# Loading q and k through casting transfers, and issuing row writes and transposes earlier, in a fused attention and MLP kernel

## Chip, cores, metric

One core of a Trainium2 chip. The metric is the device time of one execution in microseconds (us), the median of several runs. The five engines are named TensorE (PE in the profile, PEld for its weight loads), VectorE (DVE), ScalarE (ACT), GpSimd (POOL) and the sync engine (SP). SP computes nothing here; it issues transfers.

## The reference

Eight batches of eight heads, 576 tokens, head size 64, all float32. Causal attention with a decay bias comes first, then an MLP with exact GELU over all 4608 tokens.

```python
scores = scale * q @ k.T                      # per batch and head
bias   = -(cum[i] - cum[j]),  cum = cumsum(max(s, 0))
scores = where(causal, -1e9, scores + min(bias, 0))
attn   = softmax(scores);  o = attn @ v
x = o.transpose(0, 2, 1, 3).reshape(4608, 512)
y = gelu(x @ w_in) @ w_out                    # 512 -> 2048 -> 512
```

## The kernel before

The kernel works in chunks of 512 tokens. Chunk c runs the MLP of its tokens (layer 1, then layer 2) and, between the pieces of layer 2, the attention of batch c+1 (`nb`). Meanwhile the q and k of batch c+2 are prepared: loaded in float32, cast to bf16 (16 bit floats) on POOL with the two heads of a pair interleaved, written to memory as rows, and read back by transposing transfers into `qkT`. There are two `qkT` buffers, so batch c+2 takes the buffer that batch c had. Batches 0 and 1 take another way (casting loads and transposes on TensorE).

A "mask" below is VectorE's multiplication of the exponentials `P` of a block of scores by the triangle `tri_bf`; a transfer "lands" when the profile shows it complete.

The fast formula is valid only if q, k and v are small enough. A certificate checks this: `absmax` reduces each batch's `qkT`, and if the test at the end fails, a slow general branch computes everything again.

Each engine is given its instructions in the order in which the program writes them (no scheduler reorders them). What an instruction waits for is derived from the program order too.

```python
def load_qk(b, n, p0, p1, eng):                   # float32, 1536 byte runs, one slot each for q and k
    raws[b, n] = work.tile([PR, H, NR, D], fp32, tag=f"raw{n}", bufs=1, ...)
    eng.dma_start(out=raws[b, n]..., in_=...)
def cast(b, n, p, eng):                           # POOL: cast and interleave one head pair
    ... work.tile([PR, NP, NR, 2, D], bf16, tag="qkbf", bufs=2, ...)
    eng.tensor_copy(qk_of[b, i][:, p]..., raws[b, n][:, 2 * p : 2 * p + 2])
def write_rows(b, i, eng): ...                    # qk_bf -> rows in memory
def transpose_rows(b, p):                         # rows -> qkT, two transfers
    for i in range(2):
        nc.sync.dma_start_transpose(out=qkT[b % 2][:, i, p, :S], in_=rows_of[b, i][p])
def absmax(b, p):                                 # VectorE, for the certificate
    nc.vector.tensor_reduce(amx[:, b * NP + p], qkT[b % 2][:, :, p, :S], ...)

for c in range(NCH):
    nb = c + 1
    # ... first pieces of layer 1 ...
    if 0 < c and nb < B:
        if nb + 1 < B:
            load_v(nb + 1, [nc.sync])
            for i, n in enumerate("qk"):
                cast_next(nb + 1, n)              # casts, then loads q or k of batch nb+2 on POOL
                write_rows(nb + 1, i, nc.sync)
        scale_v(nb, STS, nc.vector)
        absmax_v(nb)
    # ...
    if c < B:
        for p in range(NP):
            absmax(c, p)
    for f2 in range(3, FT // 2):
        l1_item(c, f2)
    # ... c == 0 has its own order: tr_pair(1, p), load_qk(2), casts, rows and transposes of batch 2 ...
    elif nb < B:
        l2_item(c, 0, 0, 4); sc_item(nb, 0); l2_item(c, 0, 4)
        for p in range(1, NP):
            if nb + 1 < B:
                transpose_rows(nb + 1, p - 1)
            sc_item(nb, p); av_item(nb, p - 1)
            l2_item(c, p, 0, 12)                  # each finished l2 piece: copy to o_sb (3 buffers), store on SP
            # ... last p: transpose_rows(nb + 1, p), av_item(nb, p), norm_rest(nb) ...
            l2_item(c, p, 12)
```

## Time and profile before

| | before |
|---|---|
| median (lowest to highest of 3) | 351.07 us (350.35 to 351.12) |
| span of the profiled run, mean granted clock | 352.2 us, 0.985 |
| TensorE busy | 322.4 us |
| TensorE idle that is not start or tail | near 62, 88 to 95 and 182 us |
| length of chunks 1 to 6 | 41.7, 34.7, 37.8, 35.6, 34.6, 34.6 us |

A chunk's length is taken here from the start of its layer 1 in TensorE's timeline to the start of the next; 34.6 us is a chunk without a wait.

The page of the profile, the span and the engines' busy time:

```profile
span 352.2 us, 6309 instructions
...
PE 322.4 (92%) x2538; PEld 164.9 (47%) x2538; DVE 202.9 (58%) x363; ACT 202.2 (57%) x286; POOL 69.7 (20%) x98
```

The kernel is bound by TensorE, so only time in which TensorE stands still can be won. The view of waits for TensorE says what it stood still for (us in total, times, longest); the three largest lines that are not part of the start:

```profile
PE sc_ps L366 <- DMA qkT<-rows: 5.6, 2, 4.4
...
PE avr L394 <- DVE o_sb L498: 3.1, 1, 3.1
PE avd L394 <- DVE xT L427: 2.3, 1, 2.3
```

The table of stretches shows the first two with what follows: busy us of each engine (and instructions) in each stretch, then the granted clock, the DMA share and GB/s.

```profile
core 0: us, PE busy (x) PEld busy (x) DVE busy (x) ACT busy (x) POOL busy (x), PEclk, DMA share, GB/s
60.00:64.00 4.00, 0.94 (x24) 0.83 (x20) 4.00 (x6) 1.29 (x3) 3.70 (x5) 1.00 1.08 278
64.00:68.00 4.00, 4.00 (x39) 2.39 (x37) 3.96 (x6) 1.06 (x3) 3.37 (x5) 0.62 1.26 233
...
92.00:96.00 4.00, 0.58 (x8) 0.49 (x10) 0.00 (x0) 0.12 (x1) 0.00 (x0) 0.96 1.16 231
```

After a gap of some 3 us the clock was granted at 0.62 for the next 4 us, so a gap costs more than its length. In the first stretch VectorE and POOL are both busy nearly all the time: POOL casts. VectorE's timeline near the third gap shows what that does to a small mask (start, length, operation):

```profile
177.92 1.34 DVE L381 TENSOR_TENSOR P<-P,tri_bf 128x512 bf16<-128x512 bf16 x2 [0.69 <-ACT P L372]
179.18 3.70 DVE L386 TENSOR_TENSOR P<-P,tri_bf 128x128 bf16<-128x128 bf16 x1
182.81 0.41 DVE L427 SCALAR_TENSOR_TENSOR xT<-avn,ln 128x256 bf16<-128x256 f32 x1
```

This mask takes 0.22 us elsewhere. Here it took 3.70 us, to the end of four POOL casts in a row.

The groups of instructions of the reductions and of one half of the casts (busy us and mean ns, then idle time of the engine just before them and what ended it):

```profile
L203 DVE TENSOR_REDUCE amx<-qkT 128x2 f32<-128x1152 bf16 x32 | 40.9, 1335 | 0.0
...
L166 POOL CAST qk_bf<-raw_q 96x768 bf16<-96x768 f32 x24 | 20.1, 882 | 109.3 <-DMA rows<-qk_bf 102.5
```

The 0.0 on the first line is the one to remember: in the kernel before, VectorE never stood idle in front of a reduction.

Last, the transfers. The view of DMA queues from 40 to 43 us, while POOL's queue (q0: casting loads) and SP's queue (q1: v of batch 1 in 256 byte runs) are both full, gives packets, MB and share of the 16 engines:

```profile
q0 software_dynamic: 446, 0.48, 92.4%
q1 hardware_dynamic: 447, 0.11, 28.0%
```

The two queues moved packets in equal number, 446 against 447, as they would if they took turns packet by packet. A queue of small packets therefore gets little: 0.11 MB in 3 us. When POOL's queue had run empty (46 to 48 us), SP's moved 0.46 MB in 2 us.

### The profile page before, as it was taken

Reading aid. Unit: us, or ns where it says so; the run is one execution under the profiler, and the core shown is the slowest. Engines: PE = TensorE matmul, PEld = TensorE weight load, DVE = VectorE, ACT = ScalarE, POOL = GpSimd, SP = SyncE. Lnnn points to the kernel's source line nnn. Section 1 sums busy time; section 2 is a strip of 40 time slices with the busy share of each in tenths; the row PEclk is TensorE's granted clock in tenths of the full one; section 3 lists DMA queues with packets and bytes.
Section 4 is the critical chain, followed back from the end, with each engine's and each line's share of the span. In section 5 each row is a group of like instructions: output and inputs, shape, how many; then the busy total and the mean of one; then the engine's idle time right before and its main releaser. Section 6 shows DMA issues by size and latency. Waiting matters only on the chain.

```text
span 352.2 us, 6309 instructions
## 1 busy us (share of the span) xinstructions
PE 322.4 (92%) x2538; PEld 164.9 (47%) x2538; DVE 202.9 (58%) x363; ACT 202.2 (57%) x286; POOL 69.7 (20%) x98
## 2 busy tenths in 40 slices
PE   1778998798599999999979999999999999999993
PEld 1653454453255445544544455445544554444441
DVE  4596476889434985594579556865485548050011
ACT  2676628286365776667646676767576757403500
POOL 6581012705302600810080052000000000000000
PEclk9999999899989999999998999999999999999999
DMA  8999989995999999899989994862520100011011
GB/s 154 161 207 190 197 167 236 243 266 185 237 214 226 202 236 247 197 192 223 269 193 171 227 243 127 159 175 74 132 51 0 61 32 31 0 70 53 1 61 66
DMA packets 86516, 54.38 MB, mean 154 GB/s; under 512 B 67984, under 2 KB 78736, under 8 KB 86480
## 3 DMA queue, kind: packets, MB, share of 16 engines
q1 hardware_dynamic: 76752, 33.19, 42.9%
q0 software_dynamic: 9728, 20.71, 29.4%
q8 instruction: 22, 0.36, 0.4%
q14 instruction: 14, 0.11, 0.1%
HBM read 36.85 MB, written 16.52 MB: 152 GB/s over the span
## 4 chain that ended last, share of the span: by engine, by line
PE 79%; DMA 7%; DVE 6%; ACT 4%; issue 2%; SPq 1%; POOL 0%; DVEq 0%; ACTq 0%; POOLq 0%
PE o_ps L491 34%; PE h_ps L472 31%; PE sc_ps L366 5%; PE avn L394 3%; DMA rows<-qk_bf 3%; PE avd L394 3%; DMA qkT<-rows 2%; ACT P L372 2%; DVE vv L220 2%; DVE qkT L354 2%; DMA early_k<-in_k_dram 2%; PE avr L394 1%; PE tr_ps L349 1%; DVE P L381 1%; DVE P L386 1%
## 5 line engine op out<-in xcount | busy, mean ns | idle before, releaser
L491 PE MATMUL o_ps<-w_out_r,gT 128*128 128x512 bf16 x576 | 134.9, 384 | 0.0
L472 PE MATMUL h_ps<-xT,w_in_r 128*128 128x512 bf16 x576 | 127.3, 381 | 1.9 <-DVE xT L427 1.3
L472 PEld LDWEIGHTS <-w_in_r 128*128 128x128 bf16 x576 | 56.4, 98 | 70.8 <-issue 4.5
L372 ACT ACTIVATE P<-sc_ps 128x1024 bf16<-128x1024 f32 x64 | 62.0, 1021 | 47.9 <-PE sc_ps L366 47.7
L478 ACT ACTIVATE gT<-h_ps 128x1024 bf16<-128x1024 f32 x54 | 54.3, 1023 | 48.8 <-PE h_ps L472 48.7
L491 PEld LDWEIGHTS <-gT 128*128 128x128 bf16 x576 | 53.3, 98 | 61.5 <-issue 1.7
L498 DVE COPY o_sb<-o_ps 128x512 f32<-128x512 f32 x36 | 24.8, 688 | 57.9 <-PE o_ps L491 57.9
L381 DVE TENSOR_TENSOR P<-P,tri_bf 128x512 bf16<-128x512 bf16 x61 | 28.8, 475 | 49.0 <-ACT P L372 48.1
L166 POOL CAST qk_bf<-raw_q 96x768 bf16<-96x768 f32 x24 | 20.1, 882 | 109.3 <-DMA rows<-qk_bf 102.5
L203 DVE TENSOR_REDUCE amx<-qkT 128x2 f32<-128x1152 bf16 x32 | 40.9, 1335 | 0.0
L427 DVE SCALAR_TENSOR_TENSOR xT<-avn,ln 128x256 bf16<-128x256 f32 (+3 forms) x64 | 21.6, 384 | 23.3 <-ACT ln L412 23.3
L220 DVE TENSOR_TENSOR vv<-raw_v,wb 128x512 bf16<-128x512 f32 (+2 forms) x46 | 33.0, 775 | 0.0
L366 PE MATMUL sc_ps<-qkT 64*128 64x256 bf16 (+2 forms) x320 | 22.6, 267 | 9.3 <-DMA qkT<-rows 5.6
L411 ACT ACTIVATE ln<-avd 128x256 f32<-128x256 f32 x56 | 18.6, 390 | 15.2 <-PE avd L394 15.1
L366 PEld LDWEIGHTS <-qkT 64*128 64x128 bf16 x320 | 14.0, 99 | 24.2 <-issue 11.3
L412 ACT ACTIVATE ln<-ln 128x512 f32<-128x512 f32 (+1 forms) x40 | 23.5, 588 | 1.3
L394 PEld LDWEIGHTS <-vv 128*64 128x64 bf16 x384 | 18.2, 116 | 11.5 <-issue 7.7
L481 ACT ACTIVATE gT<-h_ps 128x512 bf16<-128x512 f32 x36 | 19.6, 602 | 6.3 <-PE h_ps L472 6.3
L210 DVE TENSOR_REDUCE amv<-raw_v 128x1 f32<-128x2048 f32 (+1 forms) x16 | 22.9, 1470 | 0.0
L166 POOL CAST qk_bf<-raw_k 96x768 bf16<-96x768 f32 x24 | 20.0, 880 | 0.6 <-DMA raw_k<-in_k_dram 0.6
L394 PEld LDWEIGHTS <-wb 128*64 128x64 bf16 x384 | 18.5, 117 | 2.9 <-issue 2.5
L394 PE MATMUL avd<-P,wb 128*64 128x256 bf16 x224 | 16.3, 269 | 2.3 <-DVE xT L427 2.3
(82 smaller groups left out, 154.6 us busy)
## 6 DMA issues: line engine op xcount, KB each, us to landing
out_dram<-o_sb SPq DMA_DIRECT2D x36, 256.0 KB, 2.7
raw_v<-in_v_dram SPq DMA_DIRECT2D x32, 256.0 KB, 6.7
raw_q<-in_q_dram POOLq DMA_DIRECT2D x6, 1152.0 KB, 8.6
raw_k<-in_k_dram POOLq DMA_DIRECT2D x6, 1152.0 KB, 12.3
rows<-qk_bf SPq DMA_DIRECT2D x12, 576.0 KB, 6.1
w_in_r<-in_moe_w_in_dram POOLq DMA_DIRECT2D x4, 512.0 KB, 8.0
w_out_r<-in_moe_w_out_dram POOLq DMA_DIRECT2D x4, 512.0 KB, 13.2
raw_v<-in_v_dram SPq DMA_DIRECT2D x8, 128.0 KB, 5.1
```

Of the source, the lines that this page charges most:

```text
L166: eng.tensor_copy(qk_of[b, i][:, p].rearrange("p r e d -> p e r d"), raws[b, n][:, 2 * p : 2 * p + 2])
L203: nc.vector.tensor_reduce(amx[:, b * NP + p], qkT[b % 2][:, :, p, :S], axis=AX, op=ALU.max, apply_absolute_value=True)
L220: eng.tensor_tensor(vb[:n_st, st0:st1, h0:h1, :], t[:n_st, st0:st1, h0:h1, :], wb[:n_st, st0:st1, b * H + h0 : b * H + h1] .unsqueeze(3).t ...
L366: nc.tensor.matmul(s_ps[:, e, off : off + n], lhsT=qkT[b % 2][e * 64 : e * 64 + 64, 1, p, jt * 128 : jt * 128 + 128], rhs=qkT[b % 2][e * 6 ...
L372: nc.scalar.activation(P[:, :, UO[u] : UO[u] + UW[u]], s_ps[:, :, : UW[u]], func=AF.Exp, scale=scale)
L381: eng.tensor_tensor(d, d, tri_bf.unsqueeze(1).unsqueeze(1).to_broadcast([128, 2, 2, 128]), op=MULT)
L394: nc.tensor.matmul(out[e * 64 : e * 64 + 64, lo : lo + n], lhsT=(wb[:, jt, b * H + h : b * H + h + 1].to_broadcast([128, 64]) if den else ...
L412: nc.scalar.activation(ln[:, :w], ln[:, :w], func=AF.Exp, scale=-1.0)
L472: nc.tensor.matmul(h_of[c, f2][i], lhsT=w_in_r[:, ko, ft * 128 : (ft + 1) * 128], rhs=xT[:, ko, c * NB % XW : c * NB % XW + NB], start=(ko ...
L478: nc.scalar.activation(gT_of[c][:, f2 * 2 : f2 * 2 + 2, :], hh_of[c, f2], func=AF.Gelu)
L491: nc.tensor.matmul(o_ps, lhsT=gT[:, ft, sub * 128 : (sub + 1) * 128], rhs=w_out_r[:, ft, :], start=(ft == 0), stop=(ft == FT - 1),)
L498: nc.vector.tensor_copy(o_sb, o_ps)
```

## The change

The intent: take the casts and the wide float32 loads away from POOL and the queues, and have batch c+2 ready earlier. All q and k come by the casting loads (2304 byte runs in memory, 1152 bytes in bf16), into three slots; POOL only interleaves head pairs, in bf16; batches 2 and 3 are loaded in the prologue; row writes and transposes are issued earlier. The core of the diff:

```diff
-    def load_qk(b, n, p0, p1, eng):            # float32 load, one slot
-    def cast(b, n, p, eng):                    # POOL cast, 4 per tensor
+    def load_qk(b):                            # casting loads, bufs=3
+        for p in (0, 2):
+            for n in "qk":
+                load_early(b, n, p, both=True)
+    def interleave(b, n):                      # POOL copy in bf16, 2 per tensor
 ...
+    for b in (2, 3):
+        load_qk(b)
+    for n in "qk":
+        interleave(2, n)
     for c in range(NCH):
 ...
             if nb + 1 < B:
                 load_v(nb + 1, [nc.sync])
                 for i, n in enumerate("qk"):
-                    cast_next(nb + 1, n)
+                    interleave(nb + 1, n)
                     write_rows(nb + 1, i, nc.sync)
+                if nb + 2 < B:
+                    load_qk(nb + 2)
+                for p in range(NP):
+                    transpose_rows(nb + 1, p)
             scale_v(nb, STS, nc.vector)
             absmax_v(nb)
 ...  (absmax(c, p) follows here, unchanged)
             for p in range(1, NP):
-                if nb + 1 < B:
-                    transpose_rows(nb + 1, p - 1)
                 sc_item(nb, p)
 ...  (chunk 0: both row writes of batch 2 right after load_v(2), its transposes in two places)
```

More of the change, by code (lines that the diff above doesn't have):

```diff
@@ L42 @@
     ST = 5
-    NR = 6
-    PR = S // NR
     SL = S - 512
@@ L99, in load_early @@
         src = q if n == "q" else k
-        if b == 0 and p == 0:
-            early[n] = work.tile([128, 2, 2, 2, G * D], bf16, tag=f"raw{n}", bufs=1, name=f"early_{n}")
+        if p == 0:
+            early[b, n] = work.tile([128, 2, 2, G * D], bf16, tag=f"raw{n}", bufs=3, name=f"early_{n}")
         e0 = (p // 2) * 64
-        out = early[n][e0 : e0 + 64, b, p % 2]
+        out = early[b, n][e0 : e0 + 64, p % 2]
         if both:
-            out = early[n][e0 : e0 + 64, b].rearrange("g j e f -> g (j e) f")
+            out = early[b, n][e0 : e0 + 64].rearrange("g j e f -> g (j e) f")
         ap = [[G * D, 64], [S * D, 4 if both else 2], [1, G * D]]
@@ L143 @@
     raws = {}
-    def load_qk(b, n, p0, p1, eng):
-        src = q if n == "q" else k
-        if p0 == 0:
-            raws[b, n] = work.tile([PR, H, NR, D], fp32, tag=f"raw{n}", bufs=1, name=f"raw_{n}")
-        eng.dma_start(
-            out=raws[b, n][:, 2 * p0 : 2 * p1].rearrange("p h r d -> p h (r d)"),
-            in_=bass.AP(
-                tensor=src.tensor,
-                offset=src.offset + b * H * S * D + 2 * p0 * S * D,
-                ap=[[NR * D, PR], [S * D, 2 * (p1 - p0)], [1, NR * D]],
-            ),
-        )
+    def load_qk(b):
+        for p in (0, 2):
+            for n in "qk":
+                load_early(b, n, p, both=True)
     qk_of = {}
-    def cast(b, n, p, eng):
+    def interleave(b, n):
         i = 0 if n == "q" else 1
-        if (b, i) not in qk_of:
-            qk_of[b, i] = work.tile([PR, NP, NR, 2, D], bf16, tag="qkbf", bufs=2, name="qk_bf")
-        eng.tensor_copy(
-            qk_of[b, i][:, p].rearrange("p r e d -> p e r d"), raws[b, n][:, 2 * p : 2 * p + 2]
-        )
+        t = qk_of[b, i] = work.tile([128, 2, G, 2, D], bf16, tag="qkbf", bufs=2, name="qk_bf")
+        for j in range(2):
+            nc.gpsimd.tensor_copy(
+                t[:, j].rearrange("g r e d -> g e r d"),
+                early[b, n][:, j].rearrange("g e (r d) -> g e r d", r=G),
+            )
     rows_of = {}
     def write_rows(b, i, eng):
-        rows_of[b, i] = t = dram.tile([NP, S, 128], bf16, name=f"rows{b}_{i}")
+        rows_of[b, i] = t = dram.tile([2, 2, S, 128], bf16, name=f"rows{b}_{i}")
         eng.dma_start(
-            out=t.rearrange("j (p r) c -> p j (r c)", r=NR),
+            out=t.rearrange("j a (g r) c -> (a g) j (r c)", r=G),
             in_=qk_of.pop((b, i)).rearrange("p j r e d -> p j (r e d)"),
@@ L180, in transpose_rows @@
         for i in range(2):
-            nc.sync.dma_start_transpose(out=qkT[b % 2][:, i, p, :S], in_=rows_of[b, i][p])
+            nc.sync.dma_start_transpose(out=qkT[b % 2][:, i, p, :S], in_=rows_of[b, i][p % 2, p // 2])
     def v_tile(b):
@@ L345, in tr_item @@
         e0 = (p // 2) * 64
-        src = early["qk"[i]]
+        src = early[b, "qk"[i]]
         for r in range(G):
@@ L350, in tr_item @@
                     t_ps[e * 64 : e * 64 + 64, r, :],
-                    src[e0 : e0 + 64, b, p % 2, e, r * D : (r + 1) * D],
+                    src[e0 : e0 + 64, p % 2, e, r * D : (r + 1) * D],
                     ident_bf[e0 : e0 + 64, e0 : e0 + 64],
@@ L503, in exp_set @@
         nc.scalar.preload_act_table_set("natural_log_exp_and_others")
-    def cast_next(b, n):
-        for p in range(NP):
-            cast(b, n, p, nc.gpsimd)
-        if b + 1 < B:
-            load_qk(b + 1, n, 0, NP, nc.gpsimd)
     load_v(0, [nc.sync])
@@ L551 @@
         load_w(1, i)
-    for p in (0, 2):
-        for n in "qk":
-            load_early(1, n, p, both=True)
+    load_qk(1)
     v_tile(1)
@@ L599 @@
             tr_pair(1, 3)
-            for n in "qk":
-                load_qk(2, n, 0, NP, nc.gpsimd)
             sc_item(1, 0)
@@ L604 @@
             load_v(2, [nc.sync])
-            for n in "qk":
-                cast_next(2, n)
+            for i in range(2):
+                write_rows(2, i, nc.sync)
             sc_item(1, 1)
@@ L615 @@
             l2_item(c, 3, 0, 4)
-            write_rows(2, 0, nc.sync)
+            for p in (0, 1):
+                transpose_rows(2, p)
             av_item(1, 0)
@@ L626 @@
             norm_rest(1)
-            write_rows(2, 1, nc.sync)
-            for p in range(NP):
+            for p in (2, 3):
                 transpose_rows(2, p)
@@ L643 @@
                 if p == NP - 1:
-                    if nb + 1 < B:
-                        transpose_rows(nb + 1, p)
                     av_item(nb, p)
```

## The prediction

> **What bounds it now.** TensorE: the page has it busy 322.4 us of a 352.2 us span (92%). From 113.5 us on, the chain of waits is almost wholly matmuls, 34.6 us per token chunk. What can be won:
> - (a) 60.9 to 63.9 us: TensorE waits 3.1 us for an output copy on VectorE, which POOL's casts slow (one 128x128 mask takes 0.84 us instead of 0.22). The granted clock is then 0.62 for 4 us (about 1.5 us).
> - (b) 88 to 95 us: 5.6 us for the transposes of batch 2. Their key rows, written at 74.2, landed 11.0 us later, behind the fp32 loads of batch 3. The clock falls to 0.62 again.
> - (c) 179 to 184 us: a mask waits 3.7 us, to the end of POOL's key casts; TensorE loses 3.2 us, the next chunk 1.0 us.
>
> The table by stretches has DMA near 1.0 from 24 to 221 us, so transfer order matters.
>
> **What changes.** TensorE, VectorE and ScalarE keep their order.
> - POOL: 48 casts of 0.88 us (768 elements) become 24 copies of 1152; by length 1.2 to 1.3 us each (estimate), 30 us instead of 40.
> - Loads: the same bytes are read, half written. Casting loads have 1152 byte packets (written), the fp32 loads 4.6 KB ones.
> - Loads of batches 2 and 3 follow batch 1's at once on POOL's queue, instead of waiting for 51 and 63 us.
> - SP issues rows of batch 2 right after v of batch 2, and in later chunks all eight transposes before the chunk's four output stores.
>
> **Critical path.**
> (b) goes: rows of batch 2 land near 73 us, transposes from 81, needed at 90. Gain 5.5 us.
> (c) probably goes: POOL's copies move to the start of the score phase, or before it. Gain 4 us; a contended mask may give back 1 to 2. The Trainium skill ("SBUF — State Buffer", Who interferes with whom: VectorE and GpSimd share a port pair under an exclusive lock) fits the stretched masks.
> (a) gets worse. The Trainium skill ("DMA: Bandwidth & Descriptors", Queues, rings and completion order) says that each engine round-robins between queues by packet. The trace agrees: from 34 to 46 us both queues moved about 460 packets in 3 us, so v of batch 1, in 256 byte packets, got 38 GB/s; alone (46 to 48 us) it got 0.46 MB in 2 us. Now POOL's queue stays full until about 62 us, and the last v tile lands near 61 to 62 instead of 50. VectorE, in order, waits for it at 58; TensorE resumes near 65 instead of 63.9, with the same clock dip. Loss 1 to 2 us.
> New: stores behind eight transposes. With three output buffers, in chunk 1 the fourth copy may wait for the first store's landing: 0 to 3 us.
>
> Sum: 351 − 5.5 − 4 + 1.5 + 1.5 ≈ 344.5 us. Range 338 to 351. Chances: faster 0.47, same 0.48, slower 0.05.
>
> **Right if:** no TensorE wait for transposes near 90 us; a wait of 4 us near 61 to 65 us, VectorE's v scaling waiting for its load; chunks of 34.6 us from 110 us on; no 3 us mask wait; POOL busy under 68 us.
>
> **Wrong if:** v of batch 1 lands as early as before (then nearer 341); stores hold VectorE and then TensorE for many us in chunks 1 to 4 (then 350); or POOL's copies are slower per element, or meet masks in every chunk.

## The result

| | before | after |
|---|---|---|
| median | 351.1 us (350.35 to 351.76, 4 runs) | 415.47 us (415.01 to 417.3, 4 runs) |
| ratio | | 1.1844 (95%: 1.1799 to 1.1888) |
| span, clock of the profiled run | 352.2 us, 0.985 | 413.2 us, 0.917 |
| start of chunk 1 | 71.6 us | 74.7 us |
| length of chunks 1 to 6 | 41.7, 34.7, 37.8, 35.6, 34.6, 34.6 us | 58.5, 48.0, 49.8, 42.3, 43.4, 34.6 us |

A ratio is the mean time of one kernel's fast runs over that of the other's of the same rounds, so not quite the ratio of the medians quoted. The change is 18% slower, far outside the predicted range.

The loss is in chunks 1 to 5: 16.8 + 13.3 + 12.0 + 6.8 + 8.8 = 57.7 of the 61.0 us by which the spans differ; another 3.1 us had been lost before chunk 1. These are the chunks in which the transposes of a later batch now stand ahead of the reductions (chunk 0 also transposes, but behind its reductions). Chunk 6, which prepares no batch, has its old length. TensorE's granted clock was lower there too, a mean of 0.83 to 0.92 over each of chunks 1 to 5 against 1.00 in chunk 6, so the loss contains some slower work besides waits.

The page after:

```profile
span 413.2 us, 6273 instructions
...
PE 326.3 (79%) x2496; PEld 169.7 (41%) x2538; DVE 191.2 (46%) x363; ACT 202.6 (49%) x286; POOL 61.7 (15%) x86
```

No engine was given more work than before (TensorE's busy time is 3.9 us longer, at the lower clock); all of them stand still more. The waits, all engines, the two lines that are new:

```profile
DVE amx L194 <- DMA qkT<-rows: 79.2, 17, 12.5
...
PE avn L385 <- DVE P L372: 58.9, 5, 22.3
```

TensorE waits 58.9 us in five waits for VectorE's masks, and VectorE waits 79.2 us in front of the reductions `amx`, for the transposes. The groups for the reductions and for one half of POOL's copies:

```profile
L194 DVE TENSOR_REDUCE amx<-qkT 128x2 f32<-128x1152 bf16 x32 | 42.1, 1346 | 79.2 <-DMA qkT<-rows 79.2
...
L156 POOL COPY qk_bf<-early_q 128x1152 bf16<-128x1152 bf16 x12 | 13.6, 1166 | 161.6 <-DMA rows<-qk_bf 156.9
```

The reductions are as many and as long as before (1346 against 1335 ns); the 0.0 of idle time has become 79.2. Chunk 2 shows how that reaches TensorE. VectorE's timeline there:

```profile
138.38 2.87 DVE L201 TENSOR_REDUCE amv<-raw_v 128x1 f32<-128x2048 f32 x2
149.40 1.35 DVE L194 TENSOR_REDUCE amx<-qkT 128x2 f32<-128x1152 bf16 x1 [8.14 <-DMA qkT<-rows]
154.84 1.35 DVE L194 TENSOR_REDUCE amx<-qkT 128x2 f32<-128x1152 bf16 x1 [4.09 <-DMA qkT<-rows]
160.93 2.61 DVE L194 TENSOR_REDUCE amx<-qkT 128x2 f32<-128x1152 bf16 x2 [4.74 <-DMA qkT<-rows]
163.46 0.75 DVE L372 TENSOR_TENSOR P<-P,tri_bf 128x512 bf16<-128x512 bf16 x2
```

The four reductions of chunk 2 run one by one as pairs of transposes land. Only then come the masks, which are next on VectorE and had nothing to do with the transposes. SP's timeline of the same chunk:

```profile
135.49 0.33 SPq L491 DMA_DIRECT2D out_dram<-o_sb  x1
135.87 4.64 SPq L183 DMA_DIRECT2D raw_v<-in_v_dram  x5
140.60 1.08 SPq L165 DMA_DIRECT2D rows<-qk_bf  x2
145.27 11.55 SPq L172 DMA_TRANSPOSE qkT<-rows  x8
164.97 18.81 SPq L491 DMA_DIRECT2D out_dram<-o_sb  x4
```

And the chain of waits:

```profile
148.79 2.71 PE o_ps L482 x12
...
151.81 9.03 DMA qkT<-rows
...
160.93 0.95 DVE amx L194
...
163.46 0.42 DVE P L372
...
163.93 0.95 PE avn L385 x8
```

So each chunk has become one chain: the last output store of the chunk before, v loads, rows written, rows landed, transposes, transposes landed, reductions, masks, and only then the rest of layer 2 (17.3 us, to 181.2), whose last store lets SP begin again. Transfers that were meant to be a chunk ahead are back on the critical path of the same chunk.

One part of the prediction can be read off directly: v of batch 1 starving behind POOL's queue, from 52 to 55 us.

```profile
q0 software_dynamic: 432, 0.47, 91.3%
q1 hardware_dynamic: 433, 0.11, 27.6%
```

VectorE's timeline has the v scaling waiting until 62.9 us (it was idle for the 3.52 us before, and "issue" stands there because the profile shows no releaser for it):

```profile
62.91 0.89 DVE L211 TENSOR_TENSOR vv<-raw_v,wb 128x512 bf16<-128x512 f32 x2 [3.52 <-issue]
```

### The profile page after: what moved, and what is told of

The parts are those of the page before. It is cut to its first block, busy times and chain, and to the rows that moved or that the text cites. A ratio compares the mean times of both kernels' runs of the same rounds, so it can differ in the third digit from the quotient of the medians.

```text
span 413.2 us, 6273 instructions
## 1 busy us (share of the span) xinstructions
PE 326.3 (79%) x2496; PEld 169.7 (41%) x2538; DVE 191.2 (46%) x363; ACT 202.6 (49%) x286; POOL 61.7 (15%) x86
## 4 chain that ended last, share of the span: by engine, by line
PE 62%; DMA 20%; SPq 9%; issue 3%; DVE 3%; POOL 1%; DVEq 0%
PE o_ps L482 27%; PE h_ps L463 25%; DMA qkT<-rows 8%; DMA raw_v<-in_v_dram 8%; SPq L172 5%; PE avn L385 4%; SPq L183 3%; DMA w_in_r<-in_moe_w_in_dram 3%; PE avd L385 3%; PE sc_ps L357 2%; DVE amx L194 2%; DMA rows<-qk_bf 1%; PE avr L385 1%; DVE P L372 1%; PE avw L385 1%
## 5 line engine op out<-in xcount | busy, mean ns | idle before, releaser
L482 PE MATMUL o_ps<-w_out_r,gT 128*128 128x512 bf16 x551 | 137.3, 393 | 2.7 <-issue 1.9
L463 PE MATMUL h_ps<-xT,w_in_r 128*128 128x512 bf16 x559 | 125.2, 379 | 3.1 <-DVE xT L418 1.7
L482 PEld LDWEIGHTS <-gT 128*128 128x128 bf16 x576 | 54.6, 101 | 65.7 <-issue 8.7
L194 DVE TENSOR_REDUCE amx<-qkT 128x2 f32<-128x1152 bf16 x32 | 42.1, 1346 | 79.2 <-DMA qkT<-rows 79.2
L385 PE MATMUL avn<-P,vv 128*64 128x256 bf16 x224 | 18.4, 291 | 63.4 <-DVE P L372 58.9
L385 PEld LDWEIGHTS <-vv 128*64 128x64 bf16 x384 | 20.3, 121 | 72.7 <-issue 65.2
L156 POOL COPY qk_bf<-early_q 128x1152 bf16<-128x1152 bf16 x12 | 13.6, 1166 | 161.6 <-DMA rows<-qk_bf 156.9
L372 DVE TENSOR_TENSOR P<-P,tri_bf 128x512 bf16<-128x512 bf16 x61 | 25.8, 441 | 21.7 <-ACT P L363 21.6
L211 DVE TENSOR_TENSOR vv<-raw_v,wb 128x512 bf16<-128x512 f32 (+2 forms) x46 | 26.8, 642 | 3.5 <-issue 3.5
L385 PEld LDWEIGHTS <-wb 128*64 128x64 bf16 x384 | 20.5, 125 | 0.3
L385 PE MATMUL avd<-P,wb 128*64 128x256 bf16 x224 | 18.1, 288 | 0.0
```

The source lines that it names most:

```text
L211: eng.tensor_tensor(vb[:n_st, st0:st1, h0:h1, :], t[:n_st, st0:st1, h0:h1, :], wb[:n_st, st0:st1, b * H + h0 : b * H + h1] .unsqueeze(3).t ...
L372: eng.tensor_tensor(d, d, tri_bf.unsqueeze(1).unsqueeze(1).to_broadcast([128, 2, 2, 128]), op=MULT)
L385: nc.tensor.matmul(out[e * 64 : e * 64 + 64, lo : lo + n], lhsT=(wb[:, jt, b * H + h : b * H + h + 1].to_broadcast([128, 64]) if den else ...
L463: nc.tensor.matmul(h_of[c, f2][i], lhsT=w_in_r[:, ko, ft * 128 : (ft + 1) * 128], rhs=xT[:, ko, c * NB % XW : c * NB % XW + NB], start=(ko ...
L482: nc.tensor.matmul(o_ps, lhsT=gT[:, ft, sub * 128 : (sub + 1) * 128], rhs=w_out_r[:, ft, :], start=(ft == 0), stop=(ft == FT - 1),)
```

## The experiments

**Theory R.** In chunk c the transposes of batch c+2 write the buffer that batch c had, and `absmax(c, p)` reads that buffer. Before, the reductions stood first in the program: the transposes waited for them. Now the transposes stand first, so each reduction waits for a transfer. VectorE works in order, so masks and output copies wait behind it. By the same reading the reduction no longer sees batch c at all, but batch c+2.

**Rival S.** The four output stores stand behind eight transposes on SP. Output buffers run out, and that holds VectorE and TensorE.

**Rival L.** Loads and transposes share the engines packet by packet; the many small casting packets starve the transposes.

Eleven kernels ran on the chip. In the nine timed ones chunk 6, which prepares no batch, takes 34.6 us, as before.

### e1: reductions ahead of the transposes

```diff
-                for p in range(NP):
-                    transpose_rows(nb + 1, p)
             scale_v(nb, STS, nc.vector)
             absmax_v(nb)
 ...
             for p in range(NP):
                 absmax(c, p)
+        if 0 < c and nb + 1 < B:
+            for p in range(NP):
+                transpose_rows(nb + 1, p)
```

A comparison of the two traces, without the semaphore fields, gives the same sequence of instructions on VectorE, ScalarE, GpSimd and SP and of TensorE's weight loads; TensorE's matmuls differ only in 42 records that the changed kernel's trace lacks. With the semaphore fields, VectorE's instructions differ: only the waits were changed.

> The changed kernel with the absolute-maximum reductions of chunk c written into the program ahead of the transposes of batch c+2 instead of behind them; every engine keeps exactly its order of instructions, only what waits for what differs. Theory R (the reduction reads the buffer that the transposes have just been told to fill, so VectorE waits for them, and the masks and output copies behind it wait too): VectorE's wait of 79 us for transposes goes to 0, TensorE's wait of 59 us for masks goes below 5, chunks 2 to 5 return to 34.6 us; time 340 to 347. Rival S (stores queued behind eight transposes hold the output copies): the order on SP is unchanged, so it stays near 415. Rival L (small casting packets starve the transposes): loads unchanged, stays above 400.

Measured: 347.9 us (345.47 to 349.25), ratio 0.9888 (0.9812 to 0.9965). VectorE waits for transposes no more, and TensorE's wait for masks fell from 58.9 to 2.7 us (the group of the reductions, then the view of waits):

```profile
L194 DVE TENSOR_REDUCE amx<-qkT 128x2 f32<-128x1152 bf16 x32 | 40.9, 1335 | 0.0
...
PE avn L385 <- DVE P L372: 2.7, 2, 1.9
```

Chunks 1 to 5: 34.6, 39.5, 34.6, 34.6, 34.6 us. Nearly 68 us came from the direction of one dependency, with every engine's order unchanged. S and L, as causes of the large loss, fall: SP's order and the loads are those of the slow kernel.

S survives in small. Chunk 2 has 4.8 us too many, and VectorE's timeline shows why: the fourth output copy of chunk 1 waited for a store.

```profile
108.93 0.41 DVE L418 SCALAR_TENSOR_TENSOR xT<-avr,ln 128x256 bf16<-128x256 f32 x1
116.05 0.69 DVE L489 COPY o_sb<-o_ps 128x512 f32<-128x512 f32 x1 [6.70 <-DMA out_dram<-o_sb]
```

### e2: transposes back among the pieces of layer 2

```diff
-                for p in range(NP):
-                    transpose_rows(nb + 1, p)
 ...
             for p in range(1, NP):
+                if nb + 1 < B:
+                    transpose_rows(nb + 1, p - 1)
                 sc_item(nb, p)
 ...  (and the last pair at p == NP - 1, as before)
```

> The changed kernel with only the transposes put back among the layer 2 pieces, where the kernel before had them. Theory R: the reductions precede the transposes again, so 341 to 349, within 1% of the run with the reductions first. Rival S: also falls, near 345. Rival L: stays above 400, because the loads are unchanged.

Measured: 345.92 us (344.81 to 346.41), ratio 0.9844 (0.9777 to 0.9912). Chunks 1 to 5: 34.6, 35.7, 34.6, 34.6, 34.6 us. As R expected; L is wrong again. The stores no longer stand behind the transposes, and chunk 2 lost most of its excess. The 1.1 us left fall where POOL's copies (124.0 to 128.9 us) overlap masks, one of which took 1.16 instead of 0.22 us.

### e3: the kernel before, with only its transposes moved ahead

```diff
                     cast_next(nb + 1, n)
                     write_rows(nb + 1, i, nc.sync)
+                for p in range(NP):
+                    transpose_rows(nb + 1, p)
 ...  (and removed from among the pieces of layer 2)
```

> The kernel before with only the transposes of chunks 1 to 5 moved ahead, in front of the reductions. Theory R: VectorE waits for transposes some 60 to 90 us in total, and the time is 390 to 420. Rival S: slow too. Rival L: close to 351, because the loads are those of before.

Measured: 444.89 us (442.0 and 447.78), ratio 1.2674 (1.2518 to 1.283). The move alone is enough, and without the casting loads it is worse than the change. The waits:

```profile
DVE amx L203 <- DMA qkT<-rows: 106.5, 18, 28.3
```

The direction was expected, the size was not (390 to 420 expected). Chunks 1 to 5 took 76.3, 53.4, 51.8, 44.0, 44.3 us. Chunks 2 and 3, in which POOL issues loads at the same time, are some 7 to 9 us longer than chunks 4 and 5, in which it issues none; in the changed kernel the same difference is 48.0 and 49.8 against 42.3 and 43.4 us. There the transposes of chunk 2 took 6.4 us (median) to land beside loads; those of chunk 4 took 2.6 us. So L probably has a part in the size: the chunks with loads beside transposes are about 5 to 7 us longer in the changed kernel. No run took the loads alone away, so that part is argued, not shown; it needs VectorE's wait for the transposes, for in e1 the loads are the same and those chunks lose nothing to transposes.

### e5: e1, and the loads of batch 3 behind the interleave of batch 2

This tests step (a) of the prediction, the starved v load.

```diff
-    for b in (2, 3):
-        load_qk(b)
+    load_qk(2)
     for n in "qk":
         interleave(2, n)
+    load_qk(3)
```

> The run with the reductions first, and in addition the loads of batch 3 issued after the interleave of batch 2 on POOL instead of before it, so that v of batch 1 shares the engines with one batch of loads fewer. The theory of the starved v load (a): v of batch 1 lands near 57 instead of 62.9 us, TensorE's gap near 62 to 66 us shrinks from about 4 to 1 us, the clock dip there goes, and it is 2 to 5 us faster than the run with the reductions first: 336 to 343. If the v load is not the cause, the same within 1 us.

Measured: 351.19 us (350.46 to 351.7), ratio 0.9998 (0.9931 to 1.0065). The time missed its range by 8 us, although the cause was right: TensorE's wait near 62 us fell from 4.6 to 1.5 us, the clock there stayed at 1.00 (0.65 in e1), and chunk 1 began at 69.1 instead of 73.2 us. But chunk 1 took 36.6 us and chunk 2 took 43.7. TensorE came earlier and SP did not, so the fourth output copy waited longer for its store:

```profile
118.43 0.69 DVE L489 COPY o_sb<-o_ps 128x512 f32<-128x512 f32 x1 [11.13 <-DMA out_dram<-o_sb]
```

The gain had turned into a longer wait for a store. The next three runs tested that reading.

### e7 and e8: four output buffers

e7 is e1 and e8 is e5, each with this edit:

```diff
-        o_sb = work.tile([128, KO * 128], fp32, tag="osb", bufs=3, name="o_sb")
+        o_sb = work.tile([128, KO * 128], fp32, tag="osb", bufs=4, name="o_sb")
```

> The run with the reductions first, with four output buffers instead of three. Store theory (in chunk 1 the fourth output copy waits for the landing of the first store, which stands behind eight transposes on SP): VectorE's wait of 6.7 us for the store near 109 to 116 us goes to 0, TensorE's mask waits of 2.7 us near 128 us shrink under 1, chunk 2 returns from 39.6 to about 35 us; 342 to 345.5. If the extra time of chunk 2 comes from POOL's copies meeting the masks there instead: 346 to 348.

> Reductions first, loads of batch 3 later, and four output buffers. Store theory: VectorE's wait of 11.1 us near 107 to 118 us goes, TensorE's 6.3 us mask wait near 124 to 131 us goes, chunk 2 from 43.8 to about 35 us; 339 to 343, and about 9 us faster than the same with three buffers. Otherwise 347 or more.

Measured, e7: 345.6 us (345.19 to 346.81), ratio 0.9823 (0.9768 to 0.9879), just above its range. VectorE no longer waits for a store, and chunk 2 is back from 39.5 to 34.6 us. In time it gained less than that over e1 because chunk 1 happened to begin at 75.6 instead of 73.2 us (the v load's wait was 4.1 instead of 3.2 us in this profile); the intervals of e1 and e7 overlap, the chunk lengths do not.

Measured, e8: 342.79 us (342.36 to 344.01), ratio 0.9755 (0.9712 to 0.9798), 8.4 us under e5. Chunk 2 is back from 43.7 to 34.6 us. So the store wait was what had eaten e5's gain.

### e6: e2 and the later loads of batch 3

The same question without a fourth buffer: here the stores are not behind eight transposes.

> The run with the transposes put back late, and in addition the loads of batch 3 behind the interleave of batch 2. Expected if the gain of the later load (chunk 1 began at 69.1 instead of 73.2 us) was eaten by the store queue in the run before: here the stores are not behind eight transposes, so the 3 to 5 us stay, 339 to 343. If the later load costs something of its own (rows of batch 2 land too late, batch 3 too late): 344 or more.

Measured: 341.91 us (341.48 to 343.4), ratio 0.973 (0.9687 to 0.9773). Chunk 1 begins at 68.7 us and takes 36.4 us, all later ones 34.6 us. It has the lowest median, 2.7% under the kernel before; e8 and e10 (342.79 and 342.77 us) lie within its noise. Its page:

```profile
span 339.9 us, 6262 instructions
...
PE 314.8 (93%) x2496; PEld 163.0 (48%) x2538; DVE 196.3 (58%) x363; ACT 202.1 (59%) x286; POOL 62.1 (18%) x86
```

### e9: e2 with rows and transposes of batch 2 at their old places

Step (b) of the prediction did succeed: chunk 1 fell from 41.7 to 34.6 us in e1 and e2. It has two possible causes, the earlier place of the row writes on SP, or loads that no longer stand in their way.

```diff
-            for i in range(2):
-                write_rows(2, i, nc.sync)             # right after load_v(2)
 ...
+            write_rows(2, 0, nc.sync)                 # before av_item(1, 0)
 ...
+            write_rows(2, 1, nc.sync)                 # after norm_rest(1)
+            for p in range(NP):
+                transpose_rows(2, p)
```

> The run with the transposes put back late, and in addition the row writes and transposes of batch 2 at their old, late places; the loads stay early and casting. If the wait (b) near 90 us is gone because the loads of batch 3 no longer stand in the way of the rows: the key rows land within 6 us instead of 11, TensorE waits under 1 us there, time within 1.5 us of 345.9. If it is the early place of the row writes on SP: 2 to 6 us of wait for transposes come back, 348 to 353.

Measured: 345.69 us (345.18 to 346.79), ratio 0.984 (0.9784 to 0.9896), the same as e2. TensorE does not wait for transposes. The transfers issued around the row writes: first the kernel before (69 to 75 us), then e9 (66 to 76 us); the last number is the median us from issue to landing.

```profile
rows<-qk_bf SPq DMA_DIRECT2D x2, 576.0 KB, 12.0
```

```profile
rows<-qk_bf SPq DMA_DIRECT2D x2, 576.0 KB, 3.7
```

At the old place the rows landed three times as fast: in e9 no packet of POOL's queue was moved in these 10 us, in the kernel before 214 were in its 6 us, the float32 loads of batch 3. The moved row writes gave nothing. The rest of the change gave it all, by this view the loads (earlier and casting; these two were not separated).

### e10: e6, with the certificate's decay part moved to chunk 6

e6 still has one mask wait of 1.5 us in chunk 1, behind a VectorE that works without a pause.

```diff
             absmax_v(1)
-            cert_decay()
 ...
+            if c == B - 2:
+                cert_decay()
```

> The fastest run so far (transposes late, loads of batch 3 late; 341.9 us) with the decay part of the certificate, some 2.7 us of small VectorE operations, moved from the start of chunk 1, where VectorE is busy without a pause and the first mask makes TensorE wait 1.5 us, to the end of chunk 6. If VectorE's backlog is that wait: it goes, 339 to 341.5 us. If something else sets it: 341.5 to 343.

Measured: 342.77 us (341.04 to 343.29), ratio 0.9741 (0.9685 to 0.9797): no gain. The mask wait in chunk 1 did go, and the chunk fell from 36.4 to 35.5 us, but in chunk 3 another mask wait of 0.9 us appeared and that chunk took 35.7 us. A microsecond is at the mercy of where POOL's copies meet masks.

### e11, e12, e13: what does the reduction see?

By theory R the reduction of chunk c sees batch c+2 in the changed kernel. To test that, a mark was set: one element of batch 1's q, in its buffer, after the last score of batch 1 has been read. The mark cannot reach the result. It can only reach the certificate, which then must fail and start the general branch.

```diff
             sc_item(1, 3)
+            nc.vector.memset(qkT[1][0:1, 0, 0, 0:1], 1.0e6)      # e13: 8.0
             scale_pair(1, 1)
```

> The changed kernel with a mark: after the last score of batch 1 was read, one element of batch 1's q in the buffer is set to 1e6. If chunk 1's reduction still saw batch 1, the certificate would fail and the slow general branch would run after the fast one, so the time would be far above 500 us. If it sees batch 3, as theory R says, the transposes have overwritten the mark, nothing notices it and the time stays near 416.

> The same mark in the kernel with the reductions ahead of the transposes. Theory R: the reduction sees batch 1 with its mark, the certificate fails, the general branch runs, and the time is far above 500 us, with a correct result. If the mark were never seen for another reason: near 348.

> The refused kernel with the mark set to 8 instead of 1e6, which keeps the certificate's numbers finite and is still far over its limit (8 times the largest k, some 0.4 to 0.5, against 0.375). Theory R: the reduction in chunk 1 sees batch 1 with its mark, the certificate fails, the general branch runs and the time is far above 500 us, with a correct result; near 348 if the mark is not seen.

The changed kernel with the mark (e11) took 418.77 us, one run: the mark went unnoticed. The kernel of e1 with the same mark (e12) was refused before it ran, because the certificate raises a number that contains the mark to a high power, and that overflowed. With a mark of 8 (e13) it took 2533.07 us, one run, with a correct result: the certificate failed and the general branch computed everything. The largest group of e13 is a line that only the general branch has:

```profile
L734 PE MATMUL go_ps<-gpT,g_v 128*128 128x128 f32 (+2 forms) x1920 | 626.0, 446 | 64.6 <-DVE gpT L733 64.6
```

So the order of two lines did not only cost 68 us. It also took batch 1 out of the certificate, and by the same reading of the program batch 2, while batches 6 and 7 are checked twice; for batch 2 that is argued, not run. With these inputs the results were correct in all runs.

## Why the prediction was wrong

- **The step that failed** is "TensorE, VectorE and ScalarE keep their order", used as if it said that these engines are untouched. The order was indeed unchanged. What the reductions wait for was not: 79.2 us of VectorE waits and 58.9 us of TensorE waits came of it, in the chunks that hold all but 3 us of the loss, and e1 removed them with the order still unchanged (the TensorE waits but for 2.7 us). The waits could have been listed beside the order from the start; only the order was read. The term is missing from the sum altogether.
- **Store queue ("New", 0 to 3 us).** Right in mechanism, and put in the right chunk and the right copy; in the changed kernel the larger wait hid it. In e1 it is visible: chunk 2 is 4.8 us longer than before, against 1.5 us in the sum. The term was mis-sized: in e1 the eight transposes ahead of the stores took 13.1 us to issue, and the copy waited 6.7 us.
- **(a), the v load.** Right: packets were equal in number, 432 against 433, the v scaling began at 62.9 us (61 to 62 predicted), chunk 1 began 3.1 us later than before (1 to 2 predicted), and the clock dipped to 0.58. e5 and e6 show the cause.
- **(b).** Right in effect: chunk 1 lost 7.2 us in e1 (5.5 predicted, the clock dip not counted). The reason given was half wrong: the row writes' earlier place is worth nothing (e9); what is left is the loads.
- **(c).** Right: in e1 chunks 3 and 4 are 3.2 and 1.0 us shorter than before, 4.2 us against 4 predicted. The locked port that the Trainium skill describes in "SBUF — State Buffer", Who interferes with whom, fits the stretched masks, but no run here separates it from another kind of contention.
- **POOL.** Copies of 1.17 and 1.19 us (1.2 to 1.3 predicted), POOL busy 61.7 us (under 68 predicted).

In e1 these terms add up: +1.6 (start of chunk 1) − 7.2 (chunk 1) + 4.8 (chunk 2) − 3.2 − 1.0 (chunks 3 and 4) = −5.0 us, against −4.7 us in the spans. With the missing wait taken out, 347.9 us lies within the predicted 338 to 351, 3.4 us above its middle. That it comes so near is in part luck: the store queue cost 3.3 us more than its term and (b) gave 1.7 us more, and these two misses cancel in part.

What stays open is the exact size of the loss in e3's chunk 1 (76.3 us), which was not taken apart.

## What to carry to other kernels

When a transfer is moved earlier in a program, list every access to its destination buffer that the move passes: a read that used to hold the transfer back becomes a read that waits for it, and it may read the wrong generation of the data. Compare not only the order of instructions on each engine but what each one waits for, above all on in-order engines where a needless wait holds everything behind it. And when a gain on one engine does not show in the time, look for the queue that did not move with it: here issuing a load later had let TensorE begin chunk 1 some 4 us sooner, and a store wait ate that and more until a fourth output buffer (8.4 us, e8 against e5), or stores among the transposes (9.3 us, e6 against e5), took it away.

## What the Trainium skill lacked or had wrong

- "DMA: Bandwidth & Descriptors", Queues, rings and completion order, says that each engine takes turns between queues packet by packet. The trace fits, 446 packets against 447; it shows equal numbers, not the turns, and its packets are about as long as single runs (0.11 MB/447 for v, runs of 256 bytes), where the page counts several descriptors to a packet. What it lacks is the consequence, that a queue of small packets got few bytes: a v load in 256 byte packets got 0.11 MB in 3 us (37 GB/s, 0.11/3) beside casting loads of about 1.1 KB written per packet (0.48 MB/446), and 0.46 MB in 2 us without them.
- "SBUF — State Buffer", Who interferes with whom, says that the loser of the shared port pair blocks for one instruction of the other engine. In the trace a mask of 0.22 us took 3.70 us, to the end of four POOL casts of about 0.8 us in a row. If the lock is the cause, it was not passed on between them.
- "PSUM — Partial Sum Buffer", Engine vs sequencer instructions, says that VectorE's queue is strictly first in, first out; the trace agrees, as five mask waits stood behind reductions. No page read for this case warns that the direction of a dependency follows from the place of two instructions in the program: the same order on every engine took 415.5 and 347.9 us.
- "TensorE: Matmul & The Clock Gate", What's actually happening, has the clock fall to half rate after an idle window of about 3.4 us. Here a wait of 2.3 us (kernel before, 181 to 184 us) was already followed by a mean granted clock of 0.57 over 4 us, and two waits of 1.9 and 0.9 us close together (e1, 126 to 130 us) by 0.57 too, while single waits of 1.5 and 1.4 us (e5, e6) left it at 1.00.
